# Reordering the first loads, the first sums and the opening matmuls of a fused attention and expert kernel

## The chip, the cores and the metric

The kernel runs on one core of a Trainium2 chip. Its engines are TensorE (PE in the profile, with its weight loads as PEld), VectorE (DVE), ScalarE (ACT), GpSimd (POOL) and SyncE (SP), which here issues nearly all DMAs. The metric is the device time of one execution in microseconds, lower is better. Three runs of the kernel before took 1154.9, 1155.02 and 1155.08 us; the median is 1155.02.

## The reference

Two blocks follow one another, in float32.

Linear attention with decay, over q, k, v of shape (4 batches, 8 heads, 768 positions, 64), in blocks of 64 positions:

```python
intra = np.einsum('bhic,bhjc->bhij', qb, kb) * Dmask[None]
intra = np.einsum('bhij,bhjd->bhid', intra, vb)
inter = np.einsum('bhid,bhde->bhie', qb * lam_pow[None], kv_state)
out[:, :, sl] = intra + inter
kv_state = lam_block[None, :, None, None] * kv_state + np.einsum('bhsd,bhse->bhde', kb_dec, vb)
```

Its output, as 3072 tokens of 512, is the input x of four experts, whose results are added with normalized probabilities as weights:

```python
p = domain_probs / (domain_probs.sum(-1, keepdims=True) + 1e-09)
for e in range(E):                       # E = 4, w1: 512 x 1024, w2: 1024 x 512
    h = np.maximum(x @ w1[e], 0.0)
    out += p[:, e:e + 1] * (h @ w2[e])
```

## The kernel before

The tokens are cut into chunks of 128 positions of one batch. Three groups of eight chunks (1024 tokens each) go through the four experts; a pair of a group and an expert is a unit, and there are twelve. While one unit's second product (with w2) runs on PE, the first product (with w1) of the next unit runs between its parts, and the attention of the later groups is strewn in. The work up to the end of the first unit's first product, some 87 us, has no such partner, and the change lies in its first 55 us.

Large products are made by a seven-product scheme (Strassen's, in a form with sums S1 to S4 of the left operand's blocks, T1 to T4 of the right one's, and products M1 to M7). For w1 of expert 0 the left blocks are A11, A12, A21 and A22, each 256 x 512, held as two tiles of 128 x 512, and the sums are S1 = A21 + A22, S2 = S1 - A11, S3 = A11 - A21, S4 = A12 - S2. M1 reads A11, M2 A12, M5 S1, M6 S2, M7 S3, M3 S4 and M4 A22, in that order of time (`SEQ0`). Each of the seven products is made in four quarters ("11", "12", "21", "22") by `direct_product` (line 1535; its matmuls are line 1556).

The first group's attention is three steps a chunk n: `turn(n)` (line 678) transposes q and k on PE (line 691), copies them out on ACT (699, 700) and has POOL make the decayed k, `kd`; `scores(n)` (705) has 32 small matmuls at line 721 and 32 at 728, a mask on DVE and the state's update; `values(n)` (757) makes the output at lines 775 and 793, which ACT copies into x (814).

Each engine works its instructions off in the order in which they are written. Three things set that order at the start:

- The opening (lines 500 to 528): loads of chunks 0 to 3 and of A11 and A12 on SP's queue, a few of the first on ACT's; then matmuls on a tile of zeros, whose result nobody reads. `load(n)` (160) issues six DMAs of 128 KB for a chunk, two each for q, k and v, in rows of 256 bytes. `raw_w1` (427) issues A11 and A12 as four DMAs of 128 KB in rows of 1 KB, A21 and A22 as two of 256 KB in rows of 2 KB.
- A list of slots written out by hand (lines 1634 to 1643): `ts`, `ss`, `vs` are the three attention steps of a chunk, `m1`, `m2`, `h1`, `h2` quarters and half quarters of M1 and M2, `loads` issues further loads, and `sum_first` makes one S sum on POOL as two adds of 128 x 512 (`sum_w1`, 448). `quarter_5` begins M5.
- A planner behind it: after each slot `now[0]` goes up by one and `pump()` (202) takes due work from a list of chores, by a record of how long POOL and the DMAs are taken (`busy`, `moved`, `asked`). `begin_chores` (1621) puts into it the loads and sums of w2 (`prepare_w2`, 291), whose four sums T3, T1, T2 and T4 POOL makes and SP stores.

`x_sums` (1587) makes T1 to T4 of x on DVE; the first half of T1 is made after chunk 6, the second after chunk 7.

Of the kernel before, what the change touches and what calls it, by code (L numbers as in the profile page):

```python
# [12 lines left out]
ALU = mybir.AluOpType  # L13
# [8 lines left out]
def kernel(  # L22
# [30 lines left out]
    nc = tc.nc  # L53

    B, H, S, D = q.shape
# [28 lines left out]
    half = [slice(0, D), slice(D, P)]  # L84
# [4 lines left out]
    def bank(tag, name):  # L89
        return ps.tile([P, W], FP32, name=name, tag=tag)  # L90

    def small(name):
        return pool.tile([P, W], FP32, name=name, tag="t")
# [15 lines left out]
    def send(out, in_, by=None):  # L109
        n = 4 * min(packet(out), packet(in_))  # L110
        moved[0] = max(moved[0], now[0]) + 4 * math.prod(out.shape) / n * (9 + n / 25) / 16 / 1714
        if by is None:
            asked[0] = max(asked[0], now[0]) + 0.27
        (by or nc.sync).dma_start(out=out, in_=in_)  # L114
# [35 lines left out]
    def where(n):  # L150
        g, x = divmod(n, CPG)
        return (x // 4, x % 4) if g == 0 else (2 * g + x // 2 % 2, 2 * (x // 4) + x % 2)
# [7 lines left out]
    def load(n, names="qkv"):  # L160

        c, b = where(n)
        for name in names:
            x = ({"k": acc_tile, "v": w2_tile} if n < CPG else {}).get(name, small)(f"{name}n")
            src = {"q": q, "k": k, "v": v}[name][b, :, c * C:(c + 1) * C, :]
            if name == "v":
                to, of = x[:].rearrange("p (h d) -> p h d", d=D), src.rearrange("h p d -> p h d")
                for h in (slice(0, 4), slice(4, 8)) if n < CPG else (slice(0, 8),):
                    send(out=to[:, h], in_=of[:, h], by=nc.scalar if n == 0 and h.start else None)
            else:  # L170
                to, of = x[:].rearrange("p (i r d) -> p i r d", r=2, d=D), src.rearrange("(r i) p d -> p i r d", r=2)
                for r in range(2):
                    by = nc.scalar if n == 0 and r == 1 else nc.sync
                    by.dma_start(out=to[:, :, r], in_=of[:, :, r])
            nat[n, name] = x[:].rearrange("p (h d) -> p h d", d=D)
# [26 lines left out]
    def pump(pace=1.0, force=False):  # L202
        all_added(None if force else now[0])
        while results:
            results.pop(0)()
        while late and (force or late[0][0] <= now[0]):
            late.pop(0)[1]()
        begins = chores and (
            force or free[0] <= now[0] and max(moved[0], asked[0]) < now[0] + FULL and not resting[0]
            and not (packed and busy[0] > now[0] + 1)  # L210
        )
        while queue and (force or queue[0][0] <= now[0] or begins and len(queue) > LEFT):
            queue.pop(0)[1]()
        if begins:
            begin = free[0] = max(free[0], now[0] - 1)
            was = max(busy[0], now[0])
            chores.pop(0)()
            free[0] = max(free[0], begin + max(pace * (busy[0] - was), (5 if len(chores) > 13 else 7) if spare else 1))
# [208 lines left out]
    def raw_w1(e, name, part=None):  # L427
        i, j = int(name[1]) - 1, int(name[2]) - 1
        if part == 0:
            t = stage.tile([P, 2, W], FP32, name="w1b", tag="st")  # L430
            w1_now[e][name] = t[:, 0], t[:, 1]
        if part is not None:
            for c in range(2):
                r, f = j * 256 + c * P, part * 256
                send(out=w1_now[e][name][c][:, f:f + 256], in_=moe_w1[e, r:r + P, i * W + f:i * W + f + 256])
            return
        if name in ("A21", "A22"):
            to = tuple(small("w1b")[:] for _ in range(2))
        else:
            t = stage.tile([P, 2, W], FP32, name="w1b", tag="st")  # L440
            to = t[:, 0], t[:, 1]
        for c in range(2):
            r = j * 256 + c * P
            for f in (slice(0, 256), slice(256, W)) if e == 0 and i == 0 else (slice(0, W),):
                send(out=to[c][:, f], in_=moe_w1[e, r:r + P, i * W:(i + 1) * W][:, f])
        w1_now[e][name] = to

    def sum_w1(e, name, a, b, op):
        if e == 0 or name == "S1":
            to = tuple(small("w1o")[:] for _ in range(2))  # L450
        else:
            t = stage.tile([P, 2, W], FP32, name="w1o", tag="st")
            to = t[:, 0], t[:, 1]
        for c in range(2):
            tt(nc.gpsimd, to[c], w1_now[e][a][c], w1_now[e][b][c], op)
        w1_now[e][name] = to
# [44 lines left out]
    zeros = first[:, 0:P]  # L501
# [4 lines left out]
    load(2, "qk")  # L506
    raw_w1(0, "A11", 1)
    load(2, "v")
    raw_w1(0, "A12")
    load(3)  # L510

    nc.scalar.copy(out=first[:, P:P + 1], in_=zeros[:, 0:1])

    def warm(n):
        p = bank("g1", "zp")
        for _ in range(n):
            nc.tensor.matmul(out=p[:, 0:P], lhsT=zeros, rhs=zeros, start=True, stop=True)

    def warm_small(n):
        p = [bank(t, "zp") for t in ("s0", "s1")]  # L520
        for x in range(n):
            i, o = half[x & 1], half[x >> 1 & 1]
            nc.tensor.matmul(
                out=p[x & 1][o, 0:D], lhsT=zeros[i, 0:D], rhs=zeros[i, 0:D], start=True, stop=True, skip_group_check=True,
            )

    warm_small(8)
    warm(6)

# [6 lines left out]
    for r in range(2):  # L538
        for ac in range(NHP):
            h = 4 * r + ac  # L540
            nc.vector.tensor_tensor_scan(
                out=s_decay[:, r, ac], data0=lam_bc[:, h:h + 1].to_broadcast([P, BL]), data1=blk_ident,
# [10 lines left out]
    for ac in range(NHP):  # L553
        nc.vector.tensor_tensor_scan(
            out=q_decay[:, ac], data0=lam_q[:, ac:ac + 1].to_broadcast([P, BL]), data1=zeros[:, 0:BL],
# [1031 lines left out]
    def x_sums(*halves):  # L1587

        all_added()

        for name, a, b in (("T1", "B12", "B11"), ("T2", "B22", "T1"), ("T3", "B22", "B12"), ("T4", "B21", "T2")):
            for i in range(2):
                if (name, i) not in halves:
                    continue
                tt(nc.vector, *(x_now[x][:, :, i * 256:(i + 1) * 256] for x in (name, a, b)), ALU.subtract)
# [4 lines left out]
    m1, m2 = (direct_product(m, blocks, ("g1", "g3")) for m in ("M1", "M2"))  # L1600
    m5 = []

    def quarter_5(x):
        def step():
            if not m5:
                m5.extend(direct_product("M5", blocks, ("g1", "g3")))
            m5[x]()

        return step
# [3 lines left out]
    def attend(f, n):  # L1613
        return lambda: f(n, next(pair))

    ts, ss, vs = ([attend(f, n) for n in range(CPG)] for f in (turn, scores, values))

    def sum_first(name, a, b, op=ALU.subtract):
        return lambda: sum_w1(0, name, a, b, op)
# [7 lines left out]
    def loads(*of):  # L1627
        return lambda: [raw_w1(0, x) if isinstance(x, str) else load(x) for x in of]

    def sum_x(i):  # L1630
        return lambda: x_sums(("T1", i))

    h1, h2 = parts["M1"], parts["M2"]
    for f in (
        (ts[0], lambda: warm(2)), (ss[0],), (ts[1], lambda: warm(1)), (vs[0], loads(4, 5)), (ss[1], loads("A21", 6)),
        (vs[1], loads("A22", 7)), (ts[2],), (m1[0],), (ss[2],), (m1[2],),
        (vs[2],), (ts[3],), (h2[0][0],), (ss[3],), (ts[4],), (h2[0][1],),
        (vs[3],), (h2[2][0],), (ss[4],), (ts[5],), (h2[2][1], sum_first("S3", "A11", "A21")),
        (vs[4],), (h1[1][0],), (ss[5],), (ts[6], sum_first("S1", "A21", "A22", ALU.add)), (h1[1][1],),
        (vs[5],), (h1[3][0],), (ss[6],), (ts[7], load_probs), (h1[3][1], sum_first("S2", "S1", "A11")),  # L1640
        (vs[6],), (h2[1][0], sum_x(0)), (ss[7],), (h2[1][1], sum_first("S4", "A12", "S2")),
        (begin_chores, m2[3]), (vs[7],), (sum_x(1), quarter_5(0)), (quarter_5(2),),
    ):
        for work in f:
            work()
        now[0] += 1
        pump()
# [38 lines left out]
    start, w1_steps = now[0], prepare_w1(2)  # L1686
# [26 lines left out]
    for at, (g, e) in enumerate(units):  # L1713
# [15 lines left out]
        for i in range(7):  # L1729
# [8 lines left out]
            if nests and i == 2:  # L1738
                nc.scalar.dma_start(
                    out=gate_bc, in_=gate_rows[ahead[0] - 1, :, ahead[1]].partition_broadcast(P),  # L1740
# [101 lines left out]
```

## Time and profile before

| | |
|---|---|
| median of three runs | 1155.02 us |
| the profiled execution, its own time | 1158.15 us |
| its span, from the first to the last instruction | 1156.3 us |
| PE busy in the span | 1143.0 us |
| PE busy from 0 to 60 us | 54.98 us |
| DMA share, 0 to 60 us | 0.82 |

A row of the timeline gives the start and the length of a group of equal instructions in microseconds, the engine, the line, the operation, what it writes and reads, how many there are, and in brackets the idle time of the engine ahead of it with what ended that. A float32 matmul of the program shows as two weight loads and two matmuls ("passes"), apart from transposes, which show as one of each. "Issue" means that the engine waited for no semaphore that the profile shows. In the DMA part, a queue's row gives its packets, their megabytes and their share of the 16 DMA engines' time; q1 is SP's queue, and q8 carries instructions.

### The profile page before, as it was taken

How to read it: one execution, taken by the hardware profiler on the slowest of the kernel's cores; microseconds unless marked ns; L12 is line 12 of the kernel's file. 1: busy time of each engine (PE TensorE's matmuls, PEld its weight loads, DVE VectorE, ACT ScalarE, POOL GpSimd, SP SyncE). 2: the span in 40 equal slices, each digit the busy share in tenths (PEclk: the TensorE clock that was granted, in tenths of full speed). 3: DMA queues.
4: the chain of work that ended last, by engine and by line, in shares of the span. 5: the costliest groups of instructions: out<-in, count | busy, mean ns of one | idle time of the engine just before them, and what ended most of it. 6: DMA issues, size and time to landing. Idle time of an engine off the chain costs nothing.

```text
span 1156.3 us, 22167 instructions
## 1 busy us (share of the span) xinstructions
PE 1143.0 (99%) x8015; PEld 990.3 (86%) x8015; DVE 790.0 (68%) x1428; ACT 369.8 (32%) x746; POOL 771.4 (67%) x732
## 2 busy tenths in 40 slices
PE   8999999999999999999999999999999999999998
PEld 7788888888888888888888888888888888888887
DVE  5576775477477757835775567989765566776785
ACT  4322133223312221222243442243354442342332
POOL 2748318647742974874784998894995783873884
PEclk9999999999999999999999999999999999999999
DMA  8796667999899999895957669966777756657552
GB/s 192 175 281 190 175 191 230 310 292 285 280 302 315 275 287 300 268 349 178 296 186 243 193 201 284 311 226 203 219 241 248 219 167 198 195 162 210 171 191 74
DMA packets 309148, 269.22 MB, mean 233 GB/s; under 512 B 141424, under 2 KB 244016, under 8 KB 309040
## 3 DMA queue, kind: packets, MB, share of 16 engines
q1 hardware_dynamic: 291360, 262.66, 74.0%
q10 hardware_dynamic: 17648, 5.15, 2.0%
q8 instruction: 64, 1.05, 0.4%
q14 instruction: 44, 0.36, 0.1%
q0 software_dynamic: 32, 0.00, 0.0%
HBM read 194.83 MB, written 77.10 MB: 235 GB/s over the span
## 4 chain that ended last, share of the span: by engine, by line
PE 87%; DVE 5%; POOL 3%; issue 1%; DMA 1%; SPq 1%; ACT 1%; DVEq 0%; POOLq 0%; ACTq 0%
PE pg L1096 37%; PE pq L1454 20%; PE q L1155 20%; DVE m L117 2%; PE pM L1556 2%; PE pc L1556 2%; POOL acc L117 1%; DVE sums L117 1%; PE sp L721 1%; PE op L775 1%; POOL ops L117 1%; DVE xs L117 1%; PE sp L728 1%; PE op L793 1%; SPq L114 1%
## 5 line engine op out<-in xcount | busy, mean ns | idle before, releaser
L1096 PE MATMUL pg<-xs,ws_in 128*128 128x256 f32 x1960 | 473.0, 381 | 3.7 <-DVE m L117 3.5
L1096 PEld LDWEIGHTS pg<-xs,ws_in 128*128 128x128 f32 x1960 | 369.0, 190 | 59.5 <-DVE m L117 9.5
L117 DVE TENSOR_TENSOR m<-pg,m 128x512 f32<-128x512 f32 x374 | 255.4, 686 | 104.1 <-PE pg L1096 92.0
L1155 PE MATMUL q<-w2t,m 128*128 128x256 f32 x1120 | 265.7, 380 | 0.5 <-DVE m L117 0.5
L1155 PEld LDWEIGHTS q<-w2t,m 128*128 128x128 f32 x1120 | 212.1, 190 | 29.9 <-DVE m L117 1.1
L117 POOL TENSOR_TENSOR m<-m,decay 128x512 f32<-128x512 f32 x91 | 115.4, 1283 | 89.4 <-ACT m L1113 74.0
L117 DVE TENSOR_TENSOR sums<-pq,sums 128x256 f32<-128x256 f32 x272 | 112.9, 421 | 85.5 <-PE pq L1454 75.8
L1454 PE MATMUL pq<-acc,w2t 128*128 128x256 f32 x688 | 169.3, 379 | 0.0
L1454 PEld LDWEIGHTS pq<-acc,w2t 128*128 128x128 f32 x688 | 130.7, 190 | 17.8
L1113 ACT ACTIVATE m<-m 128x512 f32<-128x512 f32 x99 | 62.4, 630 | 191.2 <-DVE m L117 191.0
L117 DVE TENSOR_TENSOR m<-m,m 128x512 f32<-128x512 f32 x112 | 103.4, 923 | 6.0 <-ACT m L1079 5.9
L1173 DVE SCALAR_TENSOR_TENSOR acc<-q,gate,acc 128x256 f32<-128x256 f32 x108 | 52.0, 481 | 73.9 <-PE q L1155 73.7
L1109 ACT COPY m<-pg 128x512 f32<-128x512 f32 x88 | 51.6, 586 | 123.8 <-PE pg L1096 119.4
L1073 ACT COPY pg<-m 128x512 f32<-128x512 f32 x77 | 45.4, 589 | 133.3 <-DVE m L117 118.7
L117 POOL TENSOR_TENSOR acc<-hT,hT 128x512 f32<-128x512 f32 x56 | 71.2, 1287 | 18.2 <-PE pq L1454 15.7
L117 POOL TENSOR_TENSOR acc<-hT,acc 128x512 f32<-128x512 f32 x56 | 71.3, 1273 | 8.5 <-PE pq L1454 4.7
L1454 PE MATMUL pq<-hT,w2t 128*128 128x256 f32 x288 | 70.0, 379 | 0.0
L117 POOL TENSOR_TENSOR w2o<-w2b 128x512 f32<-128x512 f32 x26 | 35.5, 1386 | 49.0 <-DMA w2b<-in_moe_w_dram 44.5
L1454 PEld LDWEIGHTS pq<-hT,w2t 128*128 128x128 f32 x288 | 54.5, 190 | 7.6
L1454 PE MATMUL pq<-m,w2t 128*128 128x256 f32 x228 | 55.5, 380 | 0.0
L928 ACT COPY hp<-m 128x512 f32<-128x512 f32 x84 | 48.4, 589 | 16.0 <-DVE hT L117 15.0
L117 POOL TENSOR_TENSOR xs<-xs 128x256 f32<-128x256 f32 x28 | 23.8, 849 | 44.5 <-DMA xs<-x_blocks 42.8
(149 smaller groups left out, 1438.4 us busy)
## 6 DMA issues: line engine op xcount, KB each, us to landing
w2t<-w_ops SPq DMA_DIRECT2D x129, 256.0 KB, 3.4
ws_in<-w_ops SPq DMA_DIRECT2D x40, 512.0 KB, 4.8
ws_in<-w_ops SPq DMA_DIRECT2D x60, 256.0 KB, 3.9
ws_in<-w_ops SPq DMA_DIRECT2D x40, 384.0 KB, 4.7
w2b<-in_moe_w_dram SPq DMA_DIRECT2D x56, 256.0 KB, 5.3
w_ops<-ops SPq DMA_DIRECT2D x28, 512.0 KB, 4.7
w2t<-w_sums SPq DMA_DIRECT2D x40, 256.0 KB, 4.5
w_sums<-w2o SPq DMA_DIRECT2D x16, 512.0 KB, 4.6
```

Of the source, the lines that this page charges most:

```text
L114: (by or nc.sync).dma_start(out=out, in_=in_)
L117: eng.tensor_tensor(out=o, in0=a, in1=b, op=op)
L721: nc.tensor.matmul(out=sp[r][half[x], ac * BL:(ac + 1) * BL], lhsT=hc(kT)[half[r], ac, blk[x]], rhs=hc(qT)[half[r], ac, blk[x]], start=(ac ...
L928: nc.scalar.copy(out=there[x][:], in_=blk[at][:])
L1073: nc.scalar.copy(out=banks[tags[1]][:], in_=new["11"][:])
L1096: nc.tensor.matmul(out=p[:, j * 256:(j + 1) * 256], lhsT=ws[i][:, j * P:(j + 1) * P], rhs=xs[i], start=(fresh and j == 0), stop=True, skip ...
L1109: nc.scalar.copy(out=new[at][:], in_=p[:])
L1113: nc.scalar.activation(out=new[at][:], in_=new[at][:], func=AF.Relu)
L1155: nc.tensor.matmul(out=p[:, s * DH:(s + 1) * DH], lhsT=h[A_OF[m]][:, c * 256 + s * P:c * 256 + (s + 1) * P], rhs=fed2[g, e, m][uu][:, c], ...
L1173: nc.vector.scalar_tensor_tensor(out=o, in0=x, scalar=w, in1=o, op0=ALU.mult, op1=ALU.add)
L1454: nc.tensor.matmul(out=p[:, 0:256], lhsT=fed3[e, m, x // 2][:, x % 2, c * P:(c + 1) * P], rhs=b[B_OF[i]][:, c * 256:(c + 1) * 256], start= ...
L1556: nc.tensor.matmul(out=p[:, s * 256:(s + 1) * 256], lhsT=a[c][:, f:f + P], rhs=b[:, c, j * 256:(j + 1) * 256], start=(s == 0 and c == 0 an ...
```

## The change

Four things, all in the first stretch:

- On SP's queue q and k of chunk 3 are issued ahead of A12, and v of chunk 3 behind it. Before, A12 came first and then all of chunk 3.
- A21 is issued behind chunk 7 instead of ahead of chunk 6, and A22 behind A21, one slot later, instead of ahead of chunk 7.
- The four sums on POOL, which were made in the order S3, S1, S2, S4 between the attention steps of chunks 5 to 7, are made in the order S1, S2, S3, S4, all behind the last `turn`.
- Eight matmuls of 128 x 128 on zeros open PE's work, in place of eight of 64 x 64 and six of 128 x 128.

```diff
@@ -506,8 +506,9 @@
     load(2, "qk")
     raw_w1(0, "A11", 1)
     load(2, "v")
+    load(3, "qk")
     raw_w1(0, "A12")
-    load(3)
+    load(3, "v")
@@ -516,16 +517,7 @@
-    def warm_small(n):
-        p = [bank(t, "zp") for t in ("s0", "s1")]
-        for x in range(n):
-            i, o = half[x & 1], half[x >> 1 & 1]
-            nc.tensor.matmul(
-                out=p[x & 1][o, 0:D], lhsT=zeros[i, 0:D], rhs=zeros[i, 0:D], start=True, stop=True, skip_group_check=True,
-            )
-
-    warm_small(8)
-    warm(6)
+    warm(8)
@@ -1632,14 +1624,16 @@
     for f in (
-        (ts[0], lambda: warm(2)), (ss[0],), (ts[1], lambda: warm(1)), (vs[0], loads(4, 5)), (ss[1], loads("A21", 6)),
-        (vs[1], loads("A22", 7)), (ts[2],), (m1[0],), (ss[2],), (m1[2],),
+        (ts[0], lambda: warm(2)), (ss[0],), (ts[1], lambda: warm(1)), (vs[0], loads(4, 5)), (ss[1], loads(6)),
+        (vs[1], loads(7, "A21")), (ts[2], loads("A22")), (m1[0],), (ss[2],), (m1[2],),
         (vs[2],), (ts[3],), (h2[0][0],), (ss[3],), (ts[4],), (h2[0][1],),
-        (vs[3],), (h2[2][0],), (ss[4],), (ts[5],), (h2[2][1], sum_first("S3", "A11", "A21")),
-        (vs[4],), (h1[1][0],), (ss[5],), (ts[6], sum_first("S1", "A21", "A22", ALU.add)), (h1[1][1],),
-        (vs[5],), (h1[3][0],), (ss[6],), (ts[7], load_probs), (h1[3][1], sum_first("S2", "S1", "A11")),
-        (vs[6],), (h2[1][0], sum_x(0)), (ss[7],), (h2[1][1], sum_first("S4", "A12", "S2")),
-        (begin_chores, m2[3]), (vs[7],), (sum_x(1), quarter_5(0)), (quarter_5(2),),
+        (vs[3],), (h2[2][0],), (ss[4],), (ts[5],), (h2[2][1],),
+        (vs[4],), (h1[1][0],), (ss[5],), (ts[6],), (h1[1][1],),
+        (vs[5],), (h1[3][0],), (ss[6],), (ts[7], load_probs), (h1[3][1],),
+        (vs[6],), (h2[1][0], sum_x(0), sum_first("S1", "A21", "A22", ALU.add)), (ss[7],),
+        (h2[1][1], sum_first("S2", "S1", "A11")),
+        (begin_chores, m2[3], sum_first("S3", "A11", "A21"), sum_first("S4", "A12", "S2")), (vs[7],),
+        (sum_x(1), quarter_5(0)), (quarter_5(2),),
```

## The prediction

> **What bounds the kernel now.** I read the engine shares first, then the waits of TensorE, then the timeline of the first 60 us, then the DMA issues and packets there.
>
> ```profile
> PE 1143.0 (99%) x8015; PEld 990.3 (86%) x8015; DVE 790.0 (68%) x1428; ACT 369.8 (32%) x746; POOL 771.4 (67%) x732
> ...
> q8 instruction: 64, 1.05, 0.4%
> ```
>
> PE is idle for 13.3 of 1156.3 us, so only idle time can be won, and what the change touches lies ahead of 60 us. There PE idles 5.0 us (windows 0 to 60: 54.98 busy). The timeline names the pieces:
>
> ```profile
> 22.98 0.63 PE L691 MATMUL kp<-ident,kn 128*128 128x128 f32 x4 [0.69 <-DMA kn<-in_k_dram]
> ...
> 26.06 1.06 POOL L117 TENSOR_TENSOR kd<-kn,decay 128x512 f32<-128x512 f32 x1 [1.45 <-DMA kn<-in_k_dram]
> ...
> 36.38 0.33 PE L721 MATMUL sp<-qT,kT 64*64 64x64 f32 x3 [0.91 <-issue]
> ...
> 46.02 0.33 PE L793 MATMUL op<-st,vn 64*64 64x64 f32 x5 [0.51 <-issue]
> ```
>
> The number in brackets is the idle time ahead of the row and what ended it. PE waits 0.69 us for k of chunk 3, then twice for nothing that a semaphore shows. The rest: 1.06 before the first zeros are there, 0.42 for k of chunk 0, 0.91 at 13.88 for a DVE and ACT chain, and crumbs.
>
> The loads keep the DMA engines full (share 0.8 to 1.0 in most windows up to 44 us), and SP issues each DMA only when the one eight places earlier has landed. So the landing time of a load follows from the bytes ahead of it. In the landing records k of chunk 4 is there at 25.91, of chunk 5 at 31.08, of chunk 6 at 36.90, of chunk 7 at 42.67; their transposes run at 26.04, 31.22, 37.63 and 42.97. Chunks 4 and 5 come just in time, 6 and 7 with margin.
>
> The two "issue" waits I read as PE's code. Queue q8 moved 64 blocks of 1.05 MB/64 = 16.4 KB; PE ran 8015 + 8015 + 527 semaphore instructions, 64.7 times 256. Counting PE's instructions in order of time, places 450, 1474, 1730 and 1986, all 194 above a multiple of 256, are where it pauses, and each pause ends about 1.4 us after a q8 packet: packets end at 11.21, 34.96, 40.05 and 44.67, PE goes on at 12.63, 36.38, 41.51 and 46.02. The packet that follows a crossing starts 1.6 to 2.2 us later while 256 B and 1 KB rows of the loads are under way (12.63 to 14.78, 18.57 to 20.30, 25.14 to 26.82, 41.51 to 43.09), but 3.8 and 2.8 us later at 30.10 and 36.38, when A21 and A22 with their 2 KB rows are. So I take it that a code block stands behind whatever the DMA engines have been handed, and that the wide rows hold it longest.
>
> **The change, part by part.**
>
> *Eight wide matmuls.* Out go eight small ones (1.06 to 1.70) and six wide (12 passes, 1.70 to 4.42); in come 16 wide passes from 1.06. At the spacing of the rows, 213 ns, they end near 4.63 against 4.42: the transposes of q start 0.2 later. Behind them PE waits 0.42 for k of chunk 0 (5.90) anyway, so this costs nothing; without that cover it would cost 0.2. If the passes became fast sooner, nothing is won either: the output of chunk 0 at 10.43 waits for scans on DVE that begin when lam lands (5.43). The edit also takes 24 records out of PE's stream (32 + 24 become 32), so every block border falls 24 instructions later in the work: 0.16 us where small products run, up to 0.8 among wide ones.
>
> *q and k of chunk 3 ahead of A12.* Four issues are moved past four on SP's queue. k takes the places in which A12 landed up to 18.83; with 256 B rows I allow a us more, before 20. PE asks for it at 22.29. The 0.69 goes. A12 takes the places of q and k; its third piece, the last that h2[0][0] reads, lands by 22.46, and that product would start at 22.76 (0.47 behind the transposes, as now). v keeps its place. What is late next is k of chunk 4: the bytes ahead of it are the same, it lands at 25.91 still, and PE, 0.69 early, waits that 0.69 there. Sum: 0. (Bounds: -0.69 if the load of chunk 4 comes earlier too; +0.3 if A12 lands a us late and chunk 4 with it.)
>
> *A21, A22 behind chunk 7.* Four issues of 256 KB move past eight of chunks 6 and 7. Chunk 6 loses 512 KB ahead of it, chunk 7 1 MB: 2 and 4 us at the 183 to 240 GB/s of the windows. Neither was waited for by PE, so no gain there. A22 now lands where v of chunk 7 did, near 44.6. The code blocks are what this moves. Crossing near 30.3: without A21 in the way the block takes the 4.1 to 4.8 us of the earlier ones (packet wait, packet, 1.4), there by 35.1, before PE wants it (35.7): -0.91. The next crossing, 35.7, meets chunk 7: there by 40.5, wanted at 40.7: 0. The one at 40.7 meets A21 and A22: 4.6 (as 41.51 had) to 6.3 (as 30.10 had) after it, 45.3 to 47.0, wanted at 45.9. I take the middle, 46.1: the 0.51 becomes 0.2. The one at 46.3 meets the 1 KB rows of w2 as now, 4.85 us (46.02 to 50.87): there at 51.15, wanted at 50.9: +0.2. Sum: -0.91 - 0.31 + 0.2 = -1.0, between -1.5 and +4.6 (the worst is a rival below).
>
> *S1 first on POOL.* Eight adds, 1.25 to 1.5 us each, change order; none is added. S1 starts when A22 is there (44.6) and kd of chunk 7 is done, ends near 47.1; S2 49.8, S3 52.3, S4 55.0 (2.5 to 2.9 us a pair now). M5 reads S1 from 51.4, M6 S2 from 58.9, M7 S3 from 65.8, M3 S4 from 72.8: margins of 4 us and more. Behind S4 the sums of w2 start 3.7 us later than at 51.22 and end near 66.1. SP's stores of them, at 59.46, 61.29, 63.33 and 70.67, still find them ready or wait under 0.5 us. POOL idles 5.73 us at 68.17 for a load, which takes up the rest. The planner's record of POOL is below its next due time (42 slots) in both orders, so the later order of work stays.
>
> What POOL costs is DVE:
>
> ```profile
> 58.80 2.52 DVE L117 TENSOR_TENSOR xs<-xs 128x512 f32<-128x512 f32 x2
> 61.24 1.75 DVE L117 TENSOR_TENSOR m<-m,m 128x512 f32<-128x512 f32 x1
> 62.91 0.68 DVE L117 TENSOR_TENSOR m<-pM,m 128x512 f32<-128x512 f32 x1
> 63.51 0.68 DVE L117 TENSOR_TENSOR m<-pc,m 128x512 f32<-128x512 f32 x1
> 64.11 0.68 DVE L117 TENSOR_TENSOR xs<-xs,b 128x512 f32<-128x512 f32 x1
> ```
>
> Up to 62.44, while POOL adds, DVE's operations on two SBUF tiles take up to 1.75; behind it 0.68, as those with a PSUM input always do. With POOL busy to 66.1 T3's first half (64.11) costs 1.07 more. M7 reads it at 66.77, 1.98 after it ends: hidden. T2's first half, 0.84 long, ended at 59.64 and M6 started at 59.79: no margin. If POOL holds it for the full 1.75, PE loses 0.9; if not, 0; both orders have POOL adding then, so I take +0.1. [...]
>
> **Sum.** 0 + 0 - 1.0 + 0.1 = -0.9. The profiled execution took 1158.15 (its span and 1.85 around it), which makes 1157.25; the median of the runs shown lies 3.13 below the profiled one, and from it 1155.02 - 0.9 = 1154.1. All behind 60 us is taken as PE's own pace: PE idles 8.3 us there, in DVE waits of up to 0.66, whose phase may shift by a few tenths either way.
>
> **The rivals.**
>
> *The code explanation is wrong, or the waits only move: 1155.0, 22%.* [...] As a mechanism here: if the gaps belong to the work and not to its code, they stay, and with the 0.69 handed on to chunk 4 the sum is 0.
>
> *Faster: 1152.7, 10%.* The load of chunk 4 comes earlier too, and no code block is late: 0.69 + 0.91 + 0.51 + 0.11 (41.51) + 0.12 (the DVE wait at 56.16) = 2.34. Against it: the same bytes stand ahead of chunk 4.
>
> *Slower: 1159.6, 13%.* Every block is as late as the worst seen, 6.26 us from crossing to going on (30.10 to 36.36), because the loads run denser with A21 and A22 at the end. Crossing 24.6, wanted 30.3, there 30.9; then 37.1 for 36.3, 43.4 for 42.1, 49.7 for 48.6, 55.9 for 53.7: 0.6 + 0.8 + 1.3 + 1.1 + 2.2 = 6.0, less the 1.42 of now: +4.6. It decides from about 5.2 us a block, PE's pace per 256. Against it: four of the blocks took 4.1 to 4.8.
>
> *POOL late: 1155 to 1157.5, 10%.* DVE falls back by 0.9 at M6 and by 1.07 twice more, beyond the 1.98 of margin at M7, and once the stage behind waits for a sum of own weights (POOL at 97.70, needed at 103). For it: POOL is 3.7 us later; against: 5.73 idle.
>
> **How the numbers follow.** The forecast holds 45%, with 1153.3 to 1155.2 as its own range. 0.2% is 2.3 us, about what a measurement of this kernel can tell from no change. Faster by that: the fast rival, 0.10. Slower: the slow one and some of POOL's, 0.17. Within: 0.73. The range leaves out part of the fast rival and the slow one's end: 1152.6 to 1158.0.
>
> **What would show it.** Right: no wait at the transposes of k of chunk 3, one of 0.5 to 0.7 at those of chunk 4; no "issue" gap near 36; one under 1 us near 46; S1 on POOL from 44 to 45, w2's first sum near 55; PE's M5 near 51.4. Wrong: k of chunk 4 landing away from 25.9, "issue" gaps over 1 us, or PE waiting for DVE or POOL between 52 and 75.

## The result and the profile after

The changed kernel takes 1160.62 us (median of 6 runs, 1159.63 to 1162.11) against 1155.05 us before (median of 6, 1154.19 to 1156.86): a ratio of 1.0046 [1.0033, 1.0059]. It is slower, by 5.6 us, where 1154.1 was forecast and 1158.0 was the end of the range. Its profiled execution took 1162.11 us with a span of 1160.3, against 1158.15 and 1156.3 before, so the two traces differ by 4.0 us and hold most of what the medians show; no trace shows the other 1.6 us.

The page of the changed kernel, shares of the engines:

```profile
PE 1144.5 (99%) x8003; PEld 991.4 (85%) x8003; DVE 789.6 (68%) x1428; ACT 370.9 (32%) x746; POOL 773.7 (67%) x732
```

TensorE has twelve matmuls fewer and is busy for 1.5 us longer, which a lower clock somewhere would explain. The busy time alone does not prove it: in the traces of this document without a slow clock it lies between 1140.3 and 1143.0 us, in those with one between 1141.0 and 1144.5. The waits of TensorE between 20 and 60 us:

```profile
PE sp L713 <- issue: 2.1, 1, 2.1
PE sp L720 <- issue: 1.0, 1, 1.0
PE kp L683 <- DMA kn<-in_k_dram: 0.7, 1, 0.7
PE qp L683 <- DMA qn<-in_q_dram: 0.2, 1, 0.2
```

The wait for k moved from chunk 3 to chunk 4, as forecast. The two waits for "issue" (no semaphore) did not shrink to one of 0.2 us: they are now 1.0 and 2.1. The timeline shows where:

```profile
26.38 0.63 PE L683 MATMUL kp<-ident,kn 128*128 128x128 f32 x4 [0.70 <-DMA kn<-in_k_dram]
...
36.77 0.57 PE L720 MATMUL sp<-vn,kd 64*64 64x64 f32 x23 [1.00 <-issue]
...
44.00 0.39 PE L713 MATMUL sp<-qT,kT 64*64 64x64 f32 x10 [2.11 <-issue]
```

Both pauses stand at a multiple of 256 of TensorE's instructions (plus 194, as before), called a border below. The request for a block of code is not recorded; as in the prediction, a block is taken as asked for when TensorE passes a border, and as needed at the next one. In this trace each of the nine borders from 8.63 to 55.13 us is followed by one packet of q8, which starts 0.06 to 4.75 us behind it. In these packet records, the code block asked for at 30.62 came at 33.63 to 35.16, and that asked for at 36.77 at 41.52 to 42.40: 4.75 us until its packet began. A21 and A22 were issued from 37.27 to 39.20 and landed from 41.80 to 44.38. Over all twenty traces of this document TensorE has 36 idle times of more than 0.25 us ahead of 60 us that no semaphore ends. All 36 stand at such a border, and each ends 1.27 to 1.69 us after the end of a q8 packet. That these pauses are waits for code is taken from this.

Behind the second pause the clock falls. The windows of the changed kernel (the columns are the window, its length, busy time of PE, PEld, DVE, ACT and POOL, the granted clock, the DMA share, GB/s):

```profile
42.00:44.00 2.00, 0.00 (x0) 0.00 (x0) 0.00 (x0) 0.00 (x0) 0.72 (x1) 1.00 1.16 163
44.00:46.00 2.00, 2.00 (x47) 1.88 (x47) 1.02 (x3) 0.00 (x0) 2.00 (x3) 0.65 0.52 124
46.00:48.00 2.00, 2.00 (x9) 1.67 (x7) 1.93 (x4) 1.17 (x2) 2.00 (x2) 0.50 0.56 159
```

From 42 to 44 PE, DVE and ACT all stand still, and the DMA engines are full (share 1.16). Then the clock is at half for 3.4 us (44.6 to 48.0). Before, it was 1.00 in all these windows:

```profile
42.00:44.00 2.00, 2.00 (x49) 1.88 (x39) 1.39 (x4) 0.83 (x2) 2.00 (x4) 1.00 0.95 68
44.00:46.00 2.00, 1.51 (x62) 1.04 (x61) 1.19 (x3) 0.83 (x2) 2.00 (x2) 1.00 0.55 89
46.00:48.00 2.00, 1.98 (x53) 1.53 (x56) 0.93 (x3) 0.77 (x4) 2.00 (x3) 1.00 0.96 200
```

Set against the same instructions before, the changed kernel is 0.95 us ahead at the transposes of k of chunk 3 (22.04 against 22.98), 0.33 behind at those of chunk 4, 2.43 behind after the second pause, 3.92 behind after the slow clock, and 2.73 behind from M6 on (62.52 against 59.79), because before has its own pause of 0.51 and some small waits in between.

The other 1.2 us are lost at 762 us, 700 us behind anything that the change touches. The timeline of the changed kernel there:

```profile
760.09 0.42 DVE L117 TENSOR_TENSOR sums<-pq,sums 128x256 f32<-128x256 f32 x1 [0.46 <-PE pg L1088]
760.39 1.26 POOL L117 TENSOR_TENSOR acc<-m,m 128x512 f32<-128x512 f32 x1
...
760.43 1.50 DVE L117 TENSOR_TENSOR xs<-xs 128x256 f32<-128x256 f32 x1
...
761.85 1.47 DVE L117 TENSOR_TENSOR m<-pg,m 128x512 f32<-128x512 f32 x2
762.58 1.13 PE L1088 MATMUL pg<-xs,ws_in 128*128 128x256 f32 x4 [1.15 <-DVE m L117]
```

and the same place before:

```profile
756.47 0.94 DVE L117 TENSOR_TENSOR sums<-pq,sums 128x256 f32<-128x256 f32 x2
757.33 0.63 DVE L117 TENSOR_TENSOR xs<-xs 128x256 f32<-128x256 f32 x1
757.64 1.45 POOL L117 TENSOR_TENSOR acc<-m,m 128x512 f32<-128x512 f32 x1
...
758.62 1.13 PE L1096 MATMUL pg<-xs,ws_in 128*128 128x256 f32 x4
```

Before, `xs` starts 0.31 us ahead of GpSimd's add and takes 0.63. After, the second `sums` starts 0.35 us later against the work around it, `xs` starts 0.04 behind GpSimd's add and takes 1.50, and PE waits 1.15 us for what comes next on VectorE. In these rows the one of the two that starts second takes longer: `xs` 1.50 against 0.63, GpSimd's add 1.45 against 1.26. The prediction weighed such a case at M6. A start of `xs` behind GpSimd's add, with the longer time, is called a lost turn below.

So 2.7 us come from the first stretch and 1.2 us from one lost turn. The experiments had to say why either of them happens.

### The profile page after: what moved, and what is told of

Read it like the earlier page. It is cut to its first block, busy times and chain, and to the rows that moved or that the text cites. A ratio compares the mean times of both kernels' runs of the same rounds, so it can differ in the third digit from the quotient of the medians.

```text
span 1160.3 us, 22141 instructions
## 1 busy us (share of the span) xinstructions
PE 1144.5 (99%) x8003; PEld 991.4 (85%) x8003; DVE 789.6 (68%) x1428; ACT 370.9 (32%) x746; POOL 773.7 (67%) x732
## 4 chain that ended last, share of the span: by engine, by line
PE 87%; DVE 5%; POOL 3%; SPq 2%; issue 1%; DMA 1%; ACT 1%; DVEq 0%; POOLq 0%; ACTq 0%
PE pg L1088 37%; PE pq L1446 20%; PE q L1147 20%; DVE m L117 2%; PE pM L1548 2%; PE pc L1548 2%; POOL acc L117 1%; DVE sums L117 1%; PE op L767 1%; PE sp L713 1%; SPq L174 1%; POOL ops L117 1%; PE op L785 1%; DVE xs L117 1%; PE sp L720 1%
```

## The experiments

All runs below are compared with the kernel before on the same chip. Single executions of one kernel scatter over 1152 to 1163 us there, so a verdict rests on medians and their intervals, and a trace only on whether a pause is there.

**One part at a time.** In the first batch a run undoes one part of the change (e1, e2), makes one alone (e4), or halves the rows and transfers of A21 and A22 (e3).

e1, from the changed kernel:

```diff
-(ss[1], loads(6)), (vs[1], loads(7, "A21")), (ts[2], loads("A22"))
+(ss[1], loads("A21", 6)), (vs[1], loads("A22", 7)), (ts[2],)
```

> The changed kernel with A21 ahead of chunk 6 and A22 ahead of chunk 7 again; the rest of the change stays. Theory (code behind loads: the block that PE asks for at 36.8 us waits behind A21 and A22, PE stands 2.1 us at 42 to 44, falls to half its clock for 3.4 us and loses 1.5 more): the pause at 42 is under 1 us, the clock stays at 1.00, the time is within 1.5 us of before, 1154 to 1156.5. Rival opening (24 instructions fewer ahead put a block border in a bad place): the pause stays over 1.5 us, 1159 to 1161. Rival POOL (sums late, DVE blocked): the sums are still late, 1158 or more with no pause.

Measured: 1156.36 us, 1.0005 [0.9994, 1.0015]. Waits for code of 0.79 at 35.8 and 1.01 at 41.9 (the forecast had under 1), no slow clock, no wait near 760.

e2, from the changed kernel:

```diff
-    warm(8)
+    warm_small(8)
+    warm(6)
```

(The function `warm_small` of before comes back with it.)

> The changed kernel with the opening of before, eight small and six wide matmuls; loads and sums as changed. Theory: the border comes 24 instructions earlier, 0.2 us of small products, and still meets A21 and A22: a pause of 1.5 to 2.5 us near 42, 1159 to 1161. Rival opening: the pause is gone, 1154 to 1156.

Measured: 1157.37 us, 1.0010 [0.9997, 1.0024]. No pause for code between 20 and 50 us, with A21 and A22 still behind chunk 7: the block asked for at 36.92 was there at 40.62. The wait of 1.16 us is there, at 759.2. It pauses 1.57 us at 14.0 instead, with a slow clock from 16.3 to 19.7; four of the seven later traces with the old opening do likewise (f2, which is the kernel before, e7, e8 and h2). The pause is gone, as the rival had it, but the time lies between the two forecasts.

e3, from the changed kernel:

```diff
-for f in (slice(0, 256), slice(256, W)) if e == 0 and i == 0 else (slice(0, W),):
+for f in (slice(0, 256), slice(256, W)) if e == 0 else (slice(0, W),):
```

> The changed kernel with A21 and A22 in eight DMAs of 128 KB with rows of 1 KB in place of four of 256 KB with rows of 2 KB, at the same place in SP's queue. Theory with wide rows or large DMAs as the cause: the packet of code that follows the crossing near 36.8 starts within 3 us instead of 4.75, the pause is under 0.7 us, no half clock, 1155 to 1157. If it is the place in the queue alone, whatever the size of rows and DMAs: 1159 to 1161 as the change.

Measured: 1156.66 us, 1.0005 [0.9994, 1.0016]; pauses of 1.04 at 36.0 and 1.56 at 42.7, no slow clock, no wait near 760. The time is as the theory had it, the trace is not: the packet came 3.7 us after the block was asked for (3 was the bound), and the pause is far over 0.7.

e4, from the kernel before:

```diff
-    warm_small(8)
-    warm(6)
+    warm(8)
```

> The kernel before with the eight wide matmuls alone; loads and sums as before. Theory: the borders move by 24 instructions and A21 and A22 lie where they lay, the pauses of 0.9 near 36 and 0.5 near 46 stay or change by under 0.5: 1154.5 to 1156. Rival opening: a pause of 2 us and the half clock, 1159 to 1161.

Measured: 1156.45 us, 1.0001 [0.9990, 1.0013]; no pause for code in its trace, where the forecast had the two of before staying within 0.5.

What follows: the loss is not in any one part. Taking back the place of the loads or the opening, or halving the rows, each brings the time to within 0.1% of before. That is what one expects of something that depends on when things meet, and not of a cost that a part carries with it. One caution: e1 and e3 take away two waits at once, since neither has the late one near 760; why is shown further down.

**The kernels again, and the sums.** The second batch, on another chip, has both kernels as controls (changed and unchanged source), the new order of the sums alone, and the new place of A21 and A22 with the old opening and with A12 first.

> The changed kernel, unaltered, beside the kernel before: does the loss hold on another chip, and does the same pause return? Theory (code behind A21 and A22): a pause of 1.5 us or more near 42 to 44, half clock behind it, 1159 to 1161, ratio 1.003 or more. If the pause comes by chance of one execution: ratio within 1.0015 of 1, the pause elsewhere or short.

Measured: 1160.64 us, 1.0025 [1.0013, 1.0037]. Its trace has a pause of 1.99 us at 43.37 (block asked for at 36.27, packet from 40.93) and the wait of 1.155 near 760, and no slow clock. Ahead of it stands one of 0.65 at 36.27. So the loss is real on a second chip, and about half as large.

> The kernel before, unaltered, run as if it were another: what the comparison says of no change, and a second profile of it. Ratio 0.999 to 1.001. If the pauses for code are a matter of the program alone, they stand at 36 and 46 again with 0.9 and 0.5; if of the execution, elsewhere or with other lengths.

Measured: 1157.59 us, 0.9996 [0.9987, 1.0005]. Here the kernel before pauses 1.24 us at 13.83 and has a slow clock behind it, which its first trace did not have; the pause at 36 is gone, and that at 46 is 0.78. So the pauses differ from one execution to the next. And an early pause need not cost much: this is the fastest of the run's twelve executions (1155.45). TensorE idles 2.1 us more than in the first trace ahead of 20 us, but 1.5 less from 20 to 60, where it no longer waits for k of chunk 3.

e7, from the kernel before:

```diff
-(h2[2][1], sum_first("S3", "A11", "A21")),
+(h2[2][1],),
...
-(ts[6], sum_first("S1", "A21", "A22", ALU.add)),
+(ts[6],),
...
-(h1[3][1], sum_first("S2", "S1", "A11")),
+(h1[3][1],),
...
-(h2[1][0], sum_x(0)), (ss[7],), (h2[1][1], sum_first("S4", "A12", "S2")),
+(h2[1][0], sum_x(0), sum_first("S1", "A21", "A22", ALU.add)), (ss[7],),
+(h2[1][1], sum_first("S2", "S1", "A11")),
-(begin_chores, m2[3]), (vs[7],)
+(begin_chores, m2[3], sum_first("S3", "A11", "A21"), sum_first("S4", "A12", "S2")), (vs[7],)
```

> The kernel before with the sums alone in the new order and place (S1, S2, S3, S4 behind the last transposes); loads and opening as before. Theory: the sums of w2 start 2 to 4 us later on POOL, PE loses at most 0.9 at the start of M6: 1155 to 1157.5 where before has 1156.35. Rival POOL (DVE held up by the late sums makes the loss): 3 us or more above before.

Measured: 1157.65 us, 0.9999 [0.9990, 1.0009]. Its trace pauses 1.50 us at 13.96, with a slow clock behind, and 0.51 at 46.73; there is no wait over 0.5 us near 760.

e8, from e7:

```diff
-(ss[1], loads("A21", 6)), (vs[1], loads("A22", 7)), (ts[2],)
+(ss[1], loads(6)), (vs[1], loads(7, "A21")), (ts[2], loads("A22"))
```

> The kernel before with A21 and A22 behind chunk 7 and the late sums that this needs; old opening, A12 ahead of chunk 3. Theory that these loads alone make the loss: a pause over 1.5 us between 36 and 46, 3 us or more above before. If it takes the shifted borders of the new opening too: pause under 1 us, within 1.5 us of before.

Measured: 1158.3 us, 1.0005 [0.9995, 1.0014], with pauses of 1.65 (at 13.9, with a slow clock behind), 0.98, 0.99 and 0.51 and the wait of 1.157 near 760. This one execution took 1161.71, the slowest of its twelve. Within these intervals the late sums cost nothing, and the late loads with the old opening next to nothing.

**The loads themselves.** The third batch takes away the bytes, halves the transfers, and undoes or does the part with A12.

g1, from the changed kernel, in raw_w1, leaves out the loads of A21 and A22 and makes the sums from zeros:

```diff
+            if e == 0:
+                for x in to:
+                    nc.gpsimd.memset(x, 0.0)
+                w1_now[e][name] = to
+                return
```

> The changed kernel with the four transfers of A21 and A22 (1 MB) taken out of the first stretch; GpSimd clears the two blocks' tiles instead, so the sums S1 to S4 are made from zeros and the result is not the reference's. Theory 1 (TensorE's code block asked for at 36.3 to 36.8 us waits for the data of A21 and A22): its packet starts by 39.5 us instead of 40.9 to 41.5, the pause at 43 to 44 us of 2.0 to 2.1 us shrinks to under 0.7 us, and the ratio to the kernel before falls from 1.0025 (changed kernel, second chip) to 1.0005 or less. Theory 2 (the loss lies in where GpSimd, VectorE and TensorE stand to each other later, whatever the transfers do): the ratio stays at 1.002 or more, and the wait of 1.155 us at 758 to 762 us is there.

Measured: 1157.42 us, 0.9995 [0.9983, 1.0007]. The wait at 760 is gone, but PE waits 1.26 us for VectorE at 484.4, where the kernel before waits 0.50. The waits of TensorE between 20 and 60 us:

```profile
PE sp L718 <- issue: 1.2, 2, 1.0
PE sp L725 <- issue: 0.9, 1, 0.9
PE kp L688 <- DMA kn<-in_k_dram: 0.2, 1, 0.2
```

The ratio is as theory 1 had it, the trace only in part: the block asked for at 35.92 still came at 39.66 (39.5 was the bound), and the pause is 1.0 us, not under 0.7. So in this one trace about half of the pause of 2 us is there with chunk 7 and w2 alone, without A21 and A22.

g2, from the changed kernel:

```diff
-send(out=to[c][:, f], in_=moe_w1[e, r:r + P, i * W:(i + 1) * W][:, f])
+for h in (slice(0, 64), slice(64, P)) if e == 0 and i == 1 else (slice(0, P),):
+    send(out=to[c][h, f], in_=moe_w1[e, r:r + P, i * W:(i + 1) * W][h, f])
```

> The changed kernel with A21 and A22 sent as eight transfers of 64 partitions (128 KB each), their rows still 2 KB wide. The eight transfers of 128 partitions with 1 KB rows gave a pause of 1.56 us at 42.7 and a ratio of 1.0005. Theory 1 with the number of transfers as what counts: the same here, a pause under 1.6 us and a ratio of 1.0010 or less. Theory 1 with the width of the rows as what counts: the pause stays at 2.0 us or more and the ratio at 1.0025 or more. Theory 2: the wait of 1.155 us at 758 to 762 us decides, gone with a ratio up to 1.001, there with 1.002 or more.

Measured: 1157.97 us, 0.9995 [0.9985, 1.0006]; a pause of 0.74 at 40.96, no wait near 760; an idle time of 1.11 at 243.7, which stands at no border and stays unexplained, and a wait of 0.93 for VectorE at 484.7. The prediction held the wide rows to be what delays a code block. With the same rows in smaller transfers the block was there 3.0 us after it was asked for, sooner than e3's 3.7 with rows of half the width, so in these two traces the width is not what decides.

g3, from the changed kernel:

```diff
-    load(3, "qk")
     raw_w1(0, "A12")
-    load(3, "v")
+    load(3)
```

> The changed kernel with A12 sent ahead of all of chunk 3 again (this part alone undone). The prediction's step: the 0.69 us that it gains at chunk 3 comes back as a wait for k of chunk 4, so undoing it is worth 0: a pause of about 2 us at 43 to 44 us stays, and the ratio is 1.0025 as for the changed kernel. Rival: any move of the borders of TensorE's code against the transfers by some tenths of a us decides, as it did when each other part was undone (1.0005 to 1.0010): the pause is then under 1.6 us and the ratio 1.0010 or less.

Measured: 1159.8 us, 1.0011 [0.9997, 1.0026], undecided. Its trace pauses 0.56 at 14.3, with a slow clock behind, and 0.32 at 41.6 only, and has the wait of 1.15 near 757.

e6, from the kernel before:

```diff
+    load(3, "qk")
     raw_w1(0, "A12")
-    load(3)
+    load(3, "v")
```

> The kernel before with q and k of chunk 3 sent ahead of A12, and nothing else changed. The prediction's step (0.69 us gone at chunk 3, 0.69 us back at k of chunk 4): ratio 1.0000, within 0.1%, with a wait for k of chunk 4 of 0.5 to 0.8 us near 26 us. Rival (the wait at chunk 3 is gone for good): 0.9994. Rival (code comes at other times and is paid for): 1.001 or more.

Measured: 1157.07 us, 0.9989 [0.9978, 1.0000]. No wait for k of chunk 4 near 26 us, but one of 1.78 us for k at 43.04. A gain could not be ruled out, so the run was repeated at the end.

**Why the wait at 760 us.** Seven of the profiled kernels, listed below, have exactly 1750 instruction records on VectorE (arithmetic and semaphore waits); the others have 1748, 1749, 1751 or 1754, since the waits that stand as instructions of their own are placed differently when loads move. In a stream of 1750, record 1087 (counted from 0) is the second `sums` of the rows shown above. I took that for a border of VectorE's code, as TensorE has one every 256. The six traces with 1754 records, the kernel before among them, bear this out: there record 1599, which is 512 behind 1087, starts late in the same way. Its idle time is 0.45 to 0.46 us; the same instruction has 0.11 in the other fourteen traces:

```profile
1064.64 0.69 DVE L117 TENSOR_TENSOR m<-pg,m 128x512 f32<-128x512 f32 x1 [0.46 <-PE pg L1096]
```

Both stand right behind a wait for a semaphore and start 0.42 us after that wait's record began, although the semaphore had come before. In the twenty traces no other record behind such a wait is late like this.

If the place in the stream is what counts, a test of it need touch no load: one instruction more should take the wait from the changed kernel, and two should bring it into e7. The memsets write one element in each partition, which nobody reads:

h1, from the changed kernel (1750 records become 1751):

```diff
     nc.vector.memset(zeros, 0.0)
+    nc.vector.memset(first[:, P + 2:P + 3], 0.0)
```

h2, from e7, the kernel before with late sums (1748 records become 1750):

```diff
     nc.vector.memset(zeros, 0.0)
+    nc.vector.memset(first[:, P + 2:P + 3], 0.0)
+    nc.vector.memset(first[:, P + 3:P + 4], 0.0)
```

> The changed kernel with one more instruction on VectorE: a memset of one element per partition right behind that of the zeros, which nobody reads. VectorE then has 1751 records instead of 1750. [...] The pause for TensorE's code at 43 to 44 us stays at 1.5 to 2.1 us, so the ratio to the kernel before stays over 1.000. [...]

Measured: 1158.49 us, 1.0010 [0.9995, 1.0024]; the wait is gone (0.3 us at most between 750 and 770); the median is 1.6 us below that of h3, the changed kernel in the same batch, but the intervals overlap. In its trace the pause at 43.22 is 2.78 us, the longest of all, with a slow clock behind it, and GpSimd holds PE up for 2.14 us at 436.6, which no other trace shows and which stays unexplained.

> The kernel before with the new order of the sums alone (1748 records on VectorE, ratio 0.9999, no wait of 1.155 us), and two such memsets, which make 1750 records. Theory: record 1087 falls on the sums instruction as in the changed kernel, and the wait of 1.155 us appears near 758 us in a kernel whose transfers are all where they were before; ratio about 1.001. Rival (transfers or time of day): no such wait, ratio 1.000.

Measured: 1158.82 us, 1.0012 [0.9998, 1.0025]. The wait is there, in a kernel whose loads all stand where they did before. The trace decides this; the interval of the time still includes no change:

```profile
756.23 0.42 DVE L117 TENSOR_TENSOR sums<-pq,sums 128x256 f32<-128x256 f32 x1 [0.46 <-PE pg L1098]
756.53 1.27 POOL L117 TENSOR_TENSOR acc<-m,m 128x512 f32<-128x512 f32 x1
...
756.57 1.50 DVE L117 TENSOR_TENSOR xs<-xs 128x256 f32<-128x256 f32 x1
...
758.73 1.13 PE L1098 MATMUL pg<-xs,ws_in 128*128 128x256 f32 x4 [1.16 <-DVE m L117]
```

These are the rows of the changed kernel, to within 0.01 us in length, produced by two small memsets 750 us earlier. The rival (the order of the transfers) is out. That the place in VectorE's stream decides is shown; that it is a border of its code is inferred from the places 1087 and 1599, as the records of q14, the other queue that the page names as one of instructions (0.36 MB in 44 packets on the page of the kernel before), do not say for which engine a packet is. It also explains a part of the runs above: e1, e3, g1 and g2 have 1748, 1751, 1749 and 1751 records, so each of them lost the wait near 760 besides what it was made for.

> The changed kernel a third time, as the measure for the first run of this batch: a pause of about 2 us at 43 to 44 us, a wait of 1.155 us near 760 us, and a ratio of 1.0025 to 1.0046 as on the two chips before. If both are there and the ratio is under 1.002, the two waits are not what the first chip's 5 us were.

Measured: 1160.13 us, 1.0024 [1.0009, 1.0038]. The ratio repeats, but the one execution that was profiled has neither wait (a pause of 0.71 at 46.05 and a wait of 0.92 for VectorE at 483.9 are its longest), and took 1157.86 us, 2.3 less than the median. It shows that one execution can avoid the loss without any edit. TensorE between 20 and 60 us:

```profile
PE sp L713 <- issue: 0.7, 1, 0.7
PE qp L683 <- DMA qn<-in_q_dram: 0.7, 1, 0.7
PE kp L683 <- DMA kn<-in_k_dram: 0.6, 1, 0.6
PE op L785 <- issue: 0.2, 1, 0.2
```

and VectorE at the late place:

```profile
754.62 0.41 DVE L117 TENSOR_TENSOR xs<-xs 128x256 f32<-128x256 f32 x1
754.95 0.42 DVE L117 TENSOR_TENSOR sums<-pq,sums 128x256 f32<-128x256 f32 x1
755.83 0.42 DVE L117 TENSOR_TENSOR sums<-pq,sums 128x256 f32<-128x256 f32 x1 [0.46 <-PE pq L1446]
756.16 1.50 DVE L117 TENSOR_TENSOR xs<-xs 128x256 f32<-128x256 f32 x1
```

Record 1087 is late here as well (0.46 idle) and `xs` loses its turn (1.50). But the `xs` ahead of it had won its own turn (0.41, where the changed kernel's first trace has 1.54), so VectorE was 1.1 us ahead and PE did not notice. Of the seven traces with 1750 records (the changed kernel three times, e2, e8, g3, h2) all have this `xs` of 1.50 and six have the wait; none of the thirteen others has it.

> The kernel before with the new opening and with q and k of chunk 3 ahead of A12, and with A21, A22 and the sums where they were. Alone these gave 1.0001 and 0.9989. If their parts add up: 0.9990, with a wait for k of chunk 4 of 0.5 to 0.7 us near 26 us and no pause for code over 1 us up to 50 us. If only the place of the borders of code decides, from 0.9985 to 1.0025 and a pause that the trace shows.

Measured: 1156.83 us, 0.9998 [0.9985, 1.0012], with pauses for code of 0.89 at 14.8, with a slow clock behind, and 0.74 at 42.6, and no wait for k of chunk 4. The parts do not add up to a gain.

**Both borders moved at once.** The last batch keeps the loads and sums of the change and moves only the borders: TensorE's by the old opening, VectorE's by one memset.

i1, from the changed kernel:

```diff
     nc.vector.memset(zeros, 0.0)
+    nc.vector.memset(first[:, P + 2:P + 3], 0.0)
...
-    warm(8)
+    warm_small(8)
+    warm(6)
```

> The changed kernel with the old opening (24 more records of TensorE ahead of everything, so its code borders fall earlier in the work; alone 1.0010 with the wait of 1.155 us still there) and with the one memset more on VectorE (1751 records; alone 1.0010). The transfers and the sums are where the change put them. Theory (the two code borders are the whole loss): the wait of 1.155 us is gone, no pause of 2 us at 42 to 44 us, and the ratio is 1.0000, within 0.1%. Rival (the transfers or the late sums cost something by themselves): 1.0010 or more.

Measured: 1156.77 us, 0.9992 [0.9981, 1.0003]. Its trace pauses 0.48 at 13.0 and 1.09 at 44.7, without a slow clock, and near 760 PE waits 0.4 us, as before. The interval lies clear below that of the changed kernel (1.0024 [1.0009, 1.0038] and 1.0025 [1.0013, 1.0037], each in a batch on another chip), so the moved loads and the late sums cost nothing by themselves that these intervals show, and the loss goes when both engines' streams are shifted. The old opening also displaces the work (its pause near 14 us), so that i1 and e2 do not tell the place of TensorE's border from the time at which it is reached. e2 and h1, with one border moved each, lie between (1.0010 both).

> The kernel before with q and k of chunk 3 ahead of A12, a second time, on another draw of executions. If 0.9989 was a gain of 1.2 us: 0.9985 to 0.9995. If it was scatter around the prediction's sum of 0: 0.9995 to 1.0010.

Measured: 1157.68 us, 1.0003 [0.9994, 1.0012]. The 0.9989 was scatter. No version tried is shown to beat the kernel before.

**When a block is late.** In the eight traces that send A21 and A22 behind chunk 7 in four transfers of 256 KB, the block asked for at 35 to 38 us can be set against the issue of the first of the four (the time of asking is that of the border):

| trace | asked for | first issue of A21 | ask before issue | until its packet began | next pause |
|---|---|---|---|---|---|
| h1 | 35.33 | 35.40 | 0.07 | 5.39 | 2.78 |
| f1 | 36.27 | 36.41 | 0.14 | 4.66 | 1.99 |
| changed kernel | 36.77 | 37.27 | 0.50 | 4.75 | 2.11 |
| i1 | 34.78 | 36.03 | 1.25 | 1.48 | none |
| h3 | 35.33 | 36.63 | 1.30 | 1.15 | none |
| g3 | 36.11 | 35.63 | -0.48 | 2.49 | 0.32 |
| e2 | 36.92 | 36.23 | -0.69 | 1.86 | none |
| e8 | 38.07 | 35.50 | -2.57 | 3.66 | 0.99 |

A block that is asked for up to half a us before the four are issued waits 4.7 to 5.4 us, which the work in between (about 5 us) does not cover; one asked for 1.25 us earlier waits 1.2 to 1.5, one asked for later 1.9 to 3.7. This is a pattern in eight traces. No run set the distance by itself, and what happens between the ask and the packet is not in the records, so the mechanism stays open. If it holds, it would explain why nearly any edit helps, as each moves one of the two times by some tenths of a us. The changed kernel itself stands in the table three times, with 0.14, 0.50 and 1.30: the distance differs between executions of one program.

## Why the prediction was wrong

*The opening (0): right by itself, missing one thing.* Alone it is 1.0001 (e4). The text said that it puts every border of TensorE's blocks 24 instructions later in the work, but priced that only by the crossing times; in i1, taking it back is one of the two edits that remove the loss together.

*q and k of chunk 3 ahead of A12 (0): right in the time.* In the changed kernel PE is 0.95 us ahead at chunk 3 and waits 0.70 at k of chunk 4 (0.69 forecast), which leaves it 0.33 behind; the text had +0.3 as a bound. The part alone measures 0.9989 and 1.0003, but the three traces that have it without the move of A21 and A22 (e6, i2, h4) show no wait at k of chunk 4, so there the 0.69 was not handed on in the way described.

*A21 and A22 behind chunk 7 (-1.0): this is the step that failed*, at both its terms. The block asked for near 30.3 was to take 4.1 to 4.8 us without A21 in the way; asked for at 30.62, it let PE go on at 36.77, after 6.15 us, and the pause at 36 went from 0.91 to 1.00 and not to nothing (0.65 in f1, none in h3, which run the same program). The block that met A21 and A22 was to be the one asked for at 40.7; it was the one asked for at 36.77, and it took 7.2 us (to 44.00), beyond the 6.26 that was the worst of the earlier trace. So PE stood 2.11 us for that block, where 0.2 was forecast. (A slip without effect: a chunk is six issues, so A21 moves past twelve and A22 past six, not "four past eight"; the bytes in the text are right.) The reading behind both, that the wide rows hold a block longest, fell with g2 (same rows, half the transfer: 3.0 us until the packet, 0.74 of pause) and with g1 (no A21 or A22 at all: still 3.7 us until the packet). And a fall of the clock behind the pause, 1.5 us (the lag grows from 2.43 to 3.92), was in no term, because the clock was full in the whole stretch before. What the runs put in the place of this step: the block behind the border at 36.8 came late, the clock fell behind it, and PE was 2.7 us late from M6 on instead of 0.9 early. Why the block came so late stays open.

*S1 first (+0.1): right.* e7 gives 0.9999, and the changed kernel has no wait at M6. The wait for VectorE that the text weighed there does occur elsewhere, with 0.45 to 0.77 us at 58 to 61 us in e2, e4, g2, h4 and i1; e4 and h4 have the old order of the sums, so it does not come from the order alone.

*Behind 60 us "PE's own pace", with waits whose phase "may shift by a few tenths": wrong by 1.2 us.* The steps counted instructions that the change issues, but not the semaphore waits that the new order of loads adds or takes from VectorE's stream (1754 records before, 1750 after). That brings the place 1087, taken here for a border of VectorE's code, to an instruction that has no slack, at 760 us.

*The rivals.* "Slower: 1159.6" came nearest the time, and its mechanism (late blocks with the loads denser at the end) was the right kind, but not that every block is late: one was. "The code explanation is wrong" is out: all 36 pauses stand at a border, and in the changed kernel the packets end 1.6 us before PE goes on at both pauses; for VectorE, one or two instructions more in its stream make or remove the late wait. None of the traces has more than four pauses of over 0.25 us at its 64 borders, and these stand in the first 50 us: 1.0 and 2.1 us in the changed kernel, up to 2.8 in the others. "POOL late" did not happen.

The range of 1152.6 to 1158.0 was too narrow on the slow side because it took one trace of before as what the code waits are. They change from one execution to the next: before has 0.91 and 0.51 in one trace and 1.24, with a slow clock, and 0.78 in the other; the changed kernel has 1.00 and 2.11, 0.65 and 1.99, and 0.71.

## What to carry to other kernels

Here one engine is 99% busy, its code is taken to come in blocks while it runs (64 packets of 16.4 KB on q8), and an edit of a few instructions also shifted which instruction stands at each place behind it: by 24 records on TensorE, and by 4 on VectorE (1754 to 1750, the semaphore waits counted). In such a kernel, before a small loss is put down to what an edit means to do, run it again with one or two dummy instructions on the engine that pauses: if the loss goes, the place in the stream is the first suspect. Here this test was made on VectorE alone; on TensorE the old opening moved the borders and the work together. And a forecast from one trace should take the spread of such waits from several executions, as they differ by 2 us and more in the same kernel.

## What the runs showed that was not expected

- In nine of the twenty traces the clock is at half once during the work, for 3.41 us each time. A pause of 2.1 us of PE, DVE and ACT was followed by it in the changed kernel's first trace, and one of 2.78 us in h1. Pauses of 1.24 to 1.65 us near 14 us were too (f2, e2, e7, e8, h2), and even shorter ones of 0.56 and 0.89 just behind a wait of 0.84 (g3, h4). One of 1.99 us (f1), one of 1.56 (e3) and one of 0.90 ahead of a wait of 0.91 (i2) were not. So the length of the pause does not decide it alone; what does stays open.
- Two small memsets at the start make PE wait 1.16 us at 758 us (h2), through a delay of 0.35 us and a lost turn.
- Waits for VectorE move. Where the wait near 760 is missing, a longer wait for VectorE can stand at 484 us (1.26 in g1, 0.93 in g2, 0.92 in h3; 0.50 before), so a wait that goes at one place is not always time won.
- Taking away 1 MB of loads entirely (g1) shortened the time until a code block's packet only from about 4.7 to 3.7 us.
